# Splits and sums moved from GpSimd to VectorE and ScalarE, g scaled with its clamp, and a new table of places

## The chip, the cores and the metric

The kernel runs on one core of one Trainium2 chip. The metric is the device time of one execution in microseconds. A core has five engines that matter here: TensorE (PE, matrix products; PEld is its loading of weights), VectorE (DVE), ScalarE (ACT), GpSimd (POOL) and SyncE (SP, which issues the transfers). Each takes its instructions in its own program order and waits, where an operand needs it, for another engine's semaphore.

## What is computed

Three blocks in a row: attention in which a query sees only the keys of its own hash bucket (B=2, H=8, S=768, D=64), then a gated block of width 1536, then a block of width 2048 with a piecewise activation. The weights of the last two come as float64.

```python
x = attention(q, k, v, proj)            # 1536 tokens x 512
gate = 1.0 / (1.0 + np.exp(-(x @ w_gate)))
y = gate * (x @ w_val) @ w_out          # d_ff 1536
h = y @ w_in2                           # d_ff 2048
g = np.where(h >= 1, h, np.where(h <= -1, 0.0, (h + 1) ** 2 / 4))
out = g @ w_out2
```

## The kernel before

**Products.** Every product is made of three f16 matmuls: each operand is split into a high half (a cast to f16) and a low half (what the cast left over), and hi·hi, lo·hi and hi·lo are added (lines L420 to L422, for z L1349 to L1351). So each tensor that enters a product costs one cast and one subtraction. The operands are scaled by powers of two first, which are taken from their largest absolute value. For that, a [128,1] maximum goes out to DRAM as a row (`row_out`, L255), comes back as one row, a handful of 1x1 steps make exponents of it (`exponents`, L238 to L248, two on DVE and the rest on POOL), and the result is sent out to all partitions (`row_in`, L260). The float64 weights are loaded raw and converted on chip: absolute value on ACT (L163), then clamp (L166), shift (L169), low word (L172) and sign (L175) on DVE. `w_hl` splits w_out1's and w_out2's chunks (ACT L1114, DVE L1117), `i_hi` and `i_lo` w_in2's (ACT L1152, DVE L1156).

**Stages**, by the span of the profile: attention to about 240 us; the gate and val products as "quads" (seven products for eight, on sums of blocks) to 416; w_out1 of batch 0 to about 470 and of batch 1 to 522, 12 chunks each (`o_mm`); MoE2 of batch 0, 16 chunks (`p_mm`, then `p_act`, then `z_mm`), to 661; MoE2 of batch 1 (called LB) as quads again, eight windows, to 788.

**What touches the change.** `h_hl` splits the gated h: a cast on ACT (L1162) and, on POOL, the subtraction (`xsub`, L130). `y_cp` copies w_out1's output out of PSUM (ACT L1199, DVE L1201; it is called `yf` in batch 0 and `yB` in batch 1), `y_max` takes its maxima (L1208, L1210 writes `v0s`), `y_row` fetches the scale, `y_half` (L1217 to L1221, POOL) makes the factors `usc`, and for batch 1 `y_sc` scales y in place (L1225, POOL, four times 128x768). Then 18 operations on POOL prepare batch 1's right operands: four sums (`y_sum`), seven casts (L152) and seven subtractions (L130), named B11, B21, B22 and T1 to T4. `p_act` makes g of p: relu and square on ACT (L1328, L1330), a clamp on DVE (L1333, `gg`), a scaled cast on ACT (L1338) and a scaled subtraction on DVE (L1341). `Quad2.half` does the same for batch 1 (L1294 to L1305). `g_max` (L208) takes the maxima of w_out1, w_in2 and w_out2 ahead of their use, from raw chunks called `go`, `gi` and `gz`.

**What sets the order.** No scheduler does. Each call is put into a list with a key time by `on(t, fn, ...)`, about one unit to a microsecond of TensorE's work; the list is sorted by the key and run. In the attention, `at` does the same per group of heads. So the tables of key times (AT, AM, QP, WP, YA, ZA, PA, SA, CA and the offsets in the loops) set the order of every engine.

Of the kernel before, what the change touches and what calls it, by code (L numbers as in the profile page):

```python
# [35 lines left out]
def lsh_attention_glu_act(ctx, tc, qt, kt, v, proj, w_gate, w_val, w_out1, w_in2, w_out2, ident_d, code_d, out):  # L36
# [435 lines left out]
    with ExitStack() as actx:  # L472
# [254 lines left out]
        with tc.manual_schedule():  # L727
# [895 lines left out]
```

## Time and profile before

| | us |
|---|---|
| median of 3 runs (lowest, highest) | 793.93 (792.8, 796.42) |
| the profiled execution | 794.84 |
| its span | 793.0 |

Busy time within the span: PE 738.1 us (93%), DVE 666.0 (84%), ACT 527.0 (66%), POOL 303.1 (38%). The mean granted clock of TensorE is 0.988 of full. The profile divides the span by engine, by line and by stretch; a wait of an engine is put down to the instruction of another whose end released it. Since the kernel is a chain of stages with different limits, the views by stretch are read first, then TensorE's waits in a stretch, then the timelines of the engines that it waits for.

### The profile page before, as it was taken

What the parts mean: (1) busy time and instruction counts of PE and PEld (TensorE: products, weight loads), DVE (VectorE), ACT (ScalarE), POOL (GpSimd) and SP (SyncE); (2) the same over time, 40 slices, a digit from 0 to 9 for tenths busy, and PEclk for the clock granted to TensorE, in tenths of its full rate; (3) what the DMA queues carried; (4) which work ended last, traced back from release to release, by engine and by line L of the source; (5) the groups of instructions that cost most, each with busy time, mean ns of one, the idle gap of its engine ahead of it and who ended that gap; (6) DMA issues with size and microseconds to landing.
All of it is one profiled execution on the core that took longest, in us unless ns stands there. A gap on an engine that the chain in (4) does not pass through costs nothing.

```text
span 793.0 us, 13271 instructions
## 1 busy us (share of the span) xinstructions
PE 738.1 (93%) x4883; PEld 460.9 (58%) x4883; DVE 666.0 (84%) x1106; ACT 527.0 (66%) x978; POOL 303.1 (38%) x345
## 2 busy tenths in 40 slices
PE   7899999999989999989898999988689999999997
PEld 4778888888865555555454546644245554455553
DVE  6999998988997798897789989999998895676653
ACT  6889889988866567556373445455357776776764
POOL 6334459754784445355224346306930000000000
PEclk9999999999999999999999999999889999999999
DMA  8656354534112356556568514314123300100002
GB/s 255 178 141 162 91 151 120 140 91 94 53 29 79 97 170 216 162 153 201 169 228 329 189 53 161 103 58 135 51 80 107 107 1 22 58 1 1 1 1 79
DMA packets 53200, 89.59 MB, mean 113 GB/s; under 512 B 9872, under 2 KB 33040, under 8 KB 53136
## 3 DMA queue, kind: packets, MB, share of 16 engines
q1 hardware_dynamic: 52400, 88.07, 36.7%
q8 instruction: 38, 0.62, 0.3%
q10 hardware_dynamic: 736, 0.69, 0.3%
q14 instruction: 26, 0.21, 0.1%
HBM read 68.65 MB, written 3.15 MB: 91 GB/s over the span
## 4 chain that ended last, share of the span: by engine, by line
PE 31%; DVE 23%; ACT 6%; DMA 5%; issue 4%; SPq 1%; POOL 0%; ACTq 0%; DVEq 0%
DMA wr_g<-in_moe_w_gate_dram 2%; DVE wf_o L172 2%; DVE gmx L208 2%; DVE w L172 1%; PE p L422 1%; PE p L420 1%; PE p L421 1%; PE qe L1351 1%; PE qe L1350 1%; PE qa L1350 1%; PE qe L1349 1%; PE qa L1351 1%; PE qa L1349 1%; DVE g L1341 1%; PE o L1350 1%
## 5 line engine op out<-in xcount | busy, mean ns | idle before, releaser
L642 DVE SCALAR_TENSOR_TENSOR PT<-pt,PT 128x512 f16<-128x512 f32 x144 | 95.6, 683 | 9.3 <-ACT PT L639 7.5
L604 DVE TENSOR_REDUCE st<-sc 128x1 f32<-128x768 f32 x96 | 90.9, 949 | 5.7 <-PE sc L596 4.8
L608 ACT ACTIVATE P<-sc,st 128x768 f32<-128x768 f32 x96 | 87.1, 908 | 7.6 <-DVE st L604 6.8
L639 ACT ACTIVATE PT<-pt 128x512 f16<-128x512 f32 x144 | 82.9, 600 | 12.8 <-PE pt L630 11.2
L630 PE MATMUL pt<-ident,P 128*128 128x128 f32 x576 | 80.1, 277 | 0.6 <-DVE PT L642 0.6
L630 PEld LDWEIGHTS pt<-ident,P 128*128 128x128 f32 x576 | 64.4, 140 | 13.6 <-issue 7.8
L130 POOL TENSOR_TENSOR h<-h,h 128x768 f16<-128x768 f32 x24 | 43.5, 1820 | 50.8 <-ACT h L1162 37.8
L708 PE MATMUL O<-PT,vh 128*64 128x256 f16 x576 | 54.3, 277 | 1.7 <-DVE xr L717 1.7
L420 PE MATMUL p<-y,i 128*128 128x384 f16 x128 | 43.3, 338 | 11.9 <-DVE gg L1333 10.0
L422 PE MATMUL p<-y,i 128*128 128x384 f16 x128 | 43.8, 342 | 2.7 <-DVE i L1156 2.6
L421 PE MATMUL p<-y,i 128*128 128x384 f16 x128 | 43.3, 338 | 0.0
L708 PEld LDWEIGHTS <-vh 128*64 128x64 f16 x576 | 31.0, 109 | 14.6 <-issue 13.8
L1338 ACT ACTIVATE g<-gg,usc 128x384 f16<-128x384 f32 x32 | 19.7, 615 | 29.6 <-DVE gg L1333 29.0
L1114 ACT ACTIVATE w<-wf_z,gsc 128x512 f16<-128x512 f32 x16 | 11.6, 724 | 39.7 <-DVE wf_z L175 39.7
L420 PE MATMUL y<-h,w_o 128*128 128x384 f16 x96 | 31.9, 332 | 3.5 <-DVE h L391 3.5
L708 PE MATMUL O<-PT,vl 128*64 128x256 f16 x288 | 33.8, 273 | 0.0
L1351 PEld LDWEIGHTS <-g 128*128 128x128 f16 x192 | 18.8, 98 | 23.8 <-DVE g L1341 1.0
L422 PE MATMUL y<-h,w_o 128*128 128x384 f16 x96 | 32.1, 334 | 0.0
L421 PE MATMUL y<-h,w_o 128*128 128x384 f16 x96 | 31.9, 333 | 0.0
L596 PE MATMUL sc<-N,N 128*128 128x384 f32 x96 | 28.9, 382 | 3.0 <-ACT N L532 1.9
L1114 ACT ACTIVATE w_o<-wf_o,hsc 128x512 f16<-128x512 f32 x12 | 8.7, 724 | 34.6 <-DVE wf_o L175 34.6
L1349 PEld LDWEIGHTS <-g 128*128 128x128 f16 x192 | 19.0, 99 | 21.9 <-ACT g L1338 1.6
(351 smaller groups left out, 2378.3 us busy)
## 6 DMA issues: line engine op xcount, KB each, us to landing
wr_o<-in_moe_w_out_dram SPq DMA_DIRECT2D x28, 512.0 KB, 3.9
gi<-in_moe_w_in_dram SPq DMA_DIRECT2D x21, 384.0 KB, 4.7
gz<-in_moe_w_out_dram SPq DMA_DIRECT2D x21, 384.0 KB, 5.9
go<-in_moe_w_out_dram SPq DMA_DIRECT2D x16, 384.0 KB, 4.7
H<-U SPq DMA_DIRECT2D x28, 192.0 KB, 3.4
wr_i<-in_moe_w_in_dram SPq DMA_DIRECT2D x8, 512.0 KB, 3.9
wr_i<-in_moe_w_in_dram SPq DMA_DIRECT2D x16, 256.0 KB, 3.0
n<-in_qt_dram SPq DMA_DIRECT2D x8, 384.0 KB, 4.3
```

What stands on the lines that cost most here:

```text
L130: eng.tensor_tensor(out=out, in0=a, in1=b, op=ALU.subtract)
L420: nc.tensor.matmul(ps, lhsT=wh, rhs=rh, start=first, stop=False, **kw)
L421: nc.tensor.matmul(ps, lhsT=wh, rhs=rl, start=False, stop=False, **kw)
L422: nc.tensor.matmul(ps, lhsT=wl, rhs=rh, start=False, stop=last, **kw)
L604: nc.vector.tensor_reduce(out=self.st[:, 0, self.c:self.c + 1], in_=self.sc[:, :, 0:HN], op=ALU.max, axis=AX.XY, negate=True)
L608: nc.scalar.activation(out=self.P, in_=self.sc[:, :, 0:HN], func=AF.Exp, bias=self.st[:, 0, self.c:self.c + 1], scale=1.0, accum_out=self. ...
L630: nc.tensor.transpose(self.ps[m][:, j, :], un[2 * self.n + e].P[:, a, c:c + 128], ident)
L639: nc.scalar.activation(out=self.part(0, m), in_=self.ps[m], func=AF.Copy, scale=PSCALE)
L642: nc.vector.scalar_tensor_tensor(out=self.part(1, m), in0=self.ps[m], scalar=PSCALE, in1=self.part(0, m), op0=ALU.mult, op1=ALU.subtract)
L708: nc.tensor.matmul(O_ps[r, 0:GN], lhsT=vv[m][:, e, i * D:(i + 1) * D], rhs=PT[:, l, e * NI + i, :], start=(s == 0), stop=(s == len(steps) ...
L1349: nc.tensor.matmul(OA[b][i], lhsT=gh[:, ts], rhs=wh, start=(fc == ORD2[0]), stop=False)
L1351: nc.tensor.matmul(OA[b][i], lhsT=gl[:, ts], rhs=wh, start=False, stop=(fc == ORD2[-1]))
```

## The change

It does four things.

1. `h_hl` computes the low half on DVE (24 subtractions of 128x768).
2. `y_sum` and the low halves of `y_part` move from POOL to DVE (four and seven of 128x768), the high halves from POOL to ACT (seven casts). `y_sc` stays on POOL.
3. g's scale is put into the relu's and the clamp's factors, so that the cast and the subtraction behind them have no scale operand. The factors are clamped with SMAX, for which `y_half` takes nine small POOL operations, before five.
4. The tables of key times get new numbers nearly everywhere. Beside the tables below, the y operations, which were 4.3 units apart, stand 5.26 apart; the casts and clamps of batch 0's MoE2 are 1.09 units apart, before 0.5.

```diff
@@ h_hl
-            xsub(nc.gpsimd, lo, x, hi)
+            xsub(nc.vector, lo, x, hi)
@@ y_row
-        row_in(("y", b), vmx[b][:, 4:8], 3.0, False, True)
+        row_in(("y", b), vmx[b][:, 4:8], 13.0, False, True)
@@ y_half
-        nc.gpsimd.tensor_scalar(out=usc[:, b, 4:5], in0=usc[:, b, 0:1], scalar1=2.0 ** 20, scalar2=2.0 ** -15, op0=ALU.mult, op1=ALU.max)
-        nc.gpsimd.tensor_scalar(out=usc[:, b, 0:1], in0=usc[:, b, 0:1], scalar1=2.0 ** 15, scalar2=2.0 ** -20, op0=ALU.mult, op1=ALU.min)
...
+        ts(out=u[:, 4:5], in0=u[:, 0:1], scalar1=SMAX, scalar2=1.0, op0=ALU.mult, op1=ALU.min)
+        nc.gpsimd.tensor_tensor(out=x[:, 1:2], in0=x[:, 1:2], in1=u[:, 4:5], op=ALU.mult)
+        ts(out=u[:, 0:1], in0=u[:, 0:1], scalar1=1.0, scalar2=1.0 / SMAX, op0=ALU.mult, op1=ALU.max)
...
@@ y_sum, y_part
-        b_sum(nc.gpsimd, YB, name)
+        b_sum(nc.vector, YB, name)
-            b_hi(nc.gpsimd.tensor_copy, YB, name, q2)
+            b_hi(nc.scalar.copy, YB, name, q2)
-            b_lo(nc.gpsimd, YB, name, q2)
+            b_lo(nc.vector, YB, name, q2)
@@ p_act (and alike in Quad2.half)
-            nc.scalar.activation(out=GG[b, fc][0][:, ns], in_=TT[k], func=AF.Copy, scale=u_sc(b, 0))
+            nc.scalar.copy(out=GG[b, fc][0][:, ns], in_=TT[k])
-            nc.vector.scalar_tensor_tensor(out=gl[:, ns], in0=TT[k], scalar=u_sc(b, 0), in1=gh[:, ns], op0=ALU.mult, op1=ALU.subtract)
+            xsub(nc.vector, gl[:, ns], TT[k], gh[:, ns])
@@ places
-        "v": {"seed": (1.4987, 3.9081, 5.743), "p5": 2.7931, "sum": (4.2578, 6.9331, 7.0596, 8.0394), "act": (4.894, 6.5461, 6.7413, 6.5916)},
+        "v": {"seed": (0.3623, 2.8959, 5.4602), "p5": 2.4313, "sum": (3.0782, 5.7535, 7.5389, 6.9122), "act": (3.7144, 5.3665, 5.5617, 6.5916)},
-        "v": {"load": -13.3839, "abs": (-7.5564, -5.8377), ...
+        "v": {"load": -14.3264, "abs": (-6.6935, -4.8952), ...
-            on(t0 + dt * k + 6.0, g_max, w, k)
+            on(t0 + dt * k + 6.9395, g_max, w, k)
-        for d in (-7.0, -1.8, -1.0, 0.1, 1.2, 2.4):
+        for d in (-7.4031, -2.2031, -0.9659, -0.8198, 0.7594, 1.9072):
-                    on(t0 + YA["max"][i] + (2.3 if b == LB else 0.0), y_max, b, i)
+                    on(t0 + YA["max"][i] + (1.2645 if b == LB else -1.1678), y_max, b, i)
-        on(end + 17.0 + 4.3 * i, y_sum if len(a) == 1 else y_part, *a)
+        on(end + 17.5403 + 5.2568 * i, y_sum if len(a) == 1 else y_part, *a)
```

The order that results is shown at three places. First DVE's own order in w_out1 of batch 0, one step of the loop (`wf_o` is the raw chunk under conversion, `gmx` a maximum of w_out2, `w_o` the split chunk, `h` the low half of h). Before:

```order
L172 SCALAR_TENSOR_TENSOR wf_o_5757<-wr_o_8_5696,wf_o_5757 128x512
L208 TENSOR_REDUCE gmx<-gz_5736 128x1
L175 SCALAR_TENSOR_TENSOR wf_o_5757<-wr_o_8_5696,wf_o_5757 128x512
L166 TENSOR_SCALAR wf_o_5800<-wf_o_5800 128x512
L1117 SCALAR_TENSOR_TENSOR w_o_8_5806<-wf_o_5757,hsc,w_o_8_5806 128x512
L169 TENSOR_SCALAR wf_o_5800<-wf_o_5800 128x512
L208 TENSOR_REDUCE gmx<-gz_5759 128x1
```

After:

```order
L173 SCALAR_TENSOR_TENSOR wf_o_5744<-wr_o_8_5693,wf_o_5744 128x512
L209 TENSOR_REDUCE gmx<-gz_5717 128x1
L131 TENSOR_TENSOR h_8_5783<-h_2_4293,h_8_5783 128x768
L176 SCALAR_TENSOR_TENSOR wf_o_5744<-wr_o_8_5693,wf_o_5744 128x512
L167 TENSOR_SCALAR wf_o_5788<-wf_o_5788 128x512
L209 TENSOR_REDUCE gmx<-gz_5735 128x1
L170 TENSOR_SCALAR wf_o_5788<-wf_o_5788 128x512
L1118 SCALAR_TENSOR_TENSOR w_o_8_5803<-wf_o_5744,hsc,w_o_8_5803 128x512
```

h's low half comes in between L172 and the sign step, and the clamp and shift of the next chunk now stand ahead of the low half of this one. (Lines of the changed kernel are one higher here than those of the kernel before.)

Second, DVE at the start of MoE2 of batch 0, around the last maximum of y (`vmx`, then `v0s`; `gg` is a clamped half of a chunk, `g` its low half). Before:

```order
L1333 SCALAR_TENSOR_TENSOR gg_0_1_6667<-p_0_0_1_6620,usc,t_0_1_6648 128x384
L1208 TENSOR_REDUCE vmx_68<-yB_6576 128x1
L169 TENSOR_SCALAR w_4_6645<-w_4_6645 128x512
L1341 SCALAR_TENSOR_TENSOR g_0_6643<-gg_0_1_6667,usc,g_0_6643 128x384
L1208 TENSOR_REDUCE vmx_68<-yB_6577 128x1
L1210 TENSOR_REDUCE v0s<-vmx_68 128x1
L172 SCALAR_TENSOR_TENSOR w_4_6645<-wr_i_3_6593,w_4_6645 128x512
```

After:

```order
L1209 TENSOR_REDUCE vmx_68<-yB_6580 128x1
L167 TENSOR_SCALAR w_4_6643<-w_4_6643 128x512
L1339 SCALAR_TENSOR_TENSOR gg_0_0_6666<-p_0_0_0_6606,usc,t_0_0_6640 128x384
L170 TENSOR_SCALAR w_4_6643<-w_4_6643 128x512
L1209 TENSOR_REDUCE vmx_68<-yB_6581 128x1
L1211 TENSOR_REDUCE v0s<-vmx_68 128x1
L173 SCALAR_TENSOR_TENSOR w_4_6643<-wr_i_3_6599,w_4_6643 128x512
L1339 SCALAR_TENSOR_TENSOR gg_0_1_6691<-p_0_0_1_6621,usc,t_0_1_6663 128x384
```

The maximum has moved from behind both low halves of chunk 0's g to a place ahead of its second clamp.

Third, the first of y's casts in the same stage. POOL's order before, from the last `y_sc` on (`yB` is y, `pB_y`, `pT_y` and `yT` are its parts and a sum):

```order
L1225 TENSOR_SCALAR yB_6577<-yB_6577,vmx_68 128x768
L152 CAST pB_y<-yB_6571 128x768
L130 TENSOR_TENSOR yT_6846<-yB_6572,yB_6571 128x768
L130 TENSOR_TENSOR pB_y<-yB_6571,pB_y 128x768
L152 CAST pT_y<-yT_6846 128x768
L130 TENSOR_TENSOR pT_y<-yT_6846,pT_y 128x768
```

ACT's order after, around the cast of `pB_y` (`t` is the relu and then the square of one half of a chunk, `g` its high half):

```order
L1334 ACTIVATE t_1_0_6789<-p_0_1_0_6746,usc 128x384
L1153 ACTIVATE i_9_6793<-w_1_6317,gsc 128x512
L1336 ACTIVATE t_1_0_6789<-t_1_0_6789 128x384
L1334 ACTIVATE t_1_1_6805<-p_0_1_1_6773,usc 128x384
L153 CAST pB_y<-yB_6575 128x768
L1336 ACTIVATE t_1_1_6805<-t_1_1_6805 128x384
L1344 CAST g_1_6819<-gg_1_0_6807 128x384
L164 ACTIVATE wf_z_6833<-wr_o_11_6787 128x512
```

The cast has moved from POOL, where only other work on y stood behind it, to ACT, between the relu and the square of chunk 1's second half.

## Rows read from the trace of the kernel before

**Rows 1.** Busy time of each engine by stage (instructions), then PEclk, DMA share, GB/s.

```profile
416.00:470.00 54.00, 47.28 (x271) 26.07 (x269) 48.62 (x75) 19.83 (x29) 20.25 (x14) 0.97 0.54 191
470.00:522.00 52.00, 50.17 (x309) 30.03 (x307) 46.96 (x63) 25.29 (x39) 25.86 (x24) 1.00 0.43 138
522.00:590.00 68.00, 54.37 (x260) 26.38 (x260) 64.65 (x84) 33.41 (x60) 39.19 (x31) 0.92 0.23 73
...
661.00:788.00 127.00, 125.34 (x660) 64.22 (x659) 78.97 (x138) 88.22 (x158) 0.00 (x0) 1.00 0.04 15
```

**Rows 2.** Waits of PE, 521.5 to 604: us in total, times, longest us.

```profile
PE p L420 <- DVE gg L1333: 10.0, 7, 3.6
PE p L422 <- DVE i L1156: 2.6, 5, 1.2
PE p L420 <- ACT yB L1199: 1.9, 1, 1.9
```

**Rows 3.** Waits of PE, 416 to 521.5.

```profile
PE y L420 <- DVE h L391: 3.5, 1, 3.5
PE qa L420 <- ACT w_o L1114: 1.7, 4, 0.5
PE qa L422 <- DVE w_o L1117: 1.4, 5, 0.3
```

**Rows 4.** Waits of PE, 250 to 416.

```profile
PE qb L420 <- ACT qb L385: 7.6, 5, 1.8
PE qa L420 <- DVE h L391: 2.9, 1, 2.9
```

**Rows 5.** Busy time by stretch, 388 to 392 us (columns as in rows 1).

```profile
388.00:392.00 4.00, 4.00 (x16) 2.01 (x15) 3.93 (x9) 1.23 (x3) 0.86 (x2) 0.59 0.33 67
```

**Rows 6.** Timeline of DVE, one w_out1 step: start us, us, engine, line, operation.

```profile
439.71 0.42 DVE L169 TENSOR_SCALAR wf_o<-wf_o 128x512 uint32<-128x512 uint32 x1
440.05 0.55 DVE L208 TENSOR_REDUCE gmx<-gz 128x1 f32<-128x384 f32 x1
440.51 1.67 DVE L172 SCALAR_TENSOR_TENSOR wf_o<-wr_o,wf_o 128x512 uint32<-128x512 uint32 x1
442.10 0.54 DVE L208 TENSOR_REDUCE gmx<-gz 128x1 f32<-128x384 f32 x1
442.57 0.68 DVE L175 SCALAR_TENSOR_TENSOR wf_o<-wr_o,wf_o 128x512 uint32<-128x512 uint32 x1
443.17 0.41 DVE L166 TENSOR_SCALAR wf_o<-wf_o 128x512 f32<-128x512 f32 x1
444.03 0.75 DVE L1117 SCALAR_TENSOR_TENSOR w_o<-wf_o,hsc,w_o 128x512 f16<-128x512 f32 x1 [0.45 <-ACT w_o L1114]
```

**Rows 7.** Timeline of POOL in the same step.

```profile
439.81 1.82 POOL L130 TENSOR_TENSOR h<-h,h 128x768 f16<-128x768 f32 x1 [3.17 <-ACT h L1162]
```

**Rows 8.** Groups of instructions: xcount | busy us, mean ns | idle before us.

```profile
L172 DVE SCALAR_TENSOR_TENSOR wt_g<-wr_g,wt_g 128x512 uint32<-128x512 uint32 x10 | 6.8, 680 | 0.1
L130 DVE TENSOR_TENSOR pB<-xr,pB 128x384 f16<-128x384 f32 x2 | 1.1, 552 | 1.6 <-ACT pB L152 1.6
L1162 ACT CAST h<-h 128x768 f16<-128x768 f32 x21 | 17.2, 817 | 0.0
```

**Rows 9.** Groups of instructions of DVE, 530 to 661 us.

```profile
L172 DVE SCALAR_TENSOR_TENSOR wf_z<-wr_o,wf_z 128x512 uint32<-128x512 uint32 x10 | 8.9, 891 | 0.2
```

**Rows 10.** Timeline of DVE, three reductions for y's maxima in batch 0.

```profile
473.88 2.67 DVE L1208 TENSOR_REDUCE vmx<-yf 128x1 f32<-128x768 f32 x3
```

**Rows 11.** Timeline of ACT ahead of the wait at 522.

```profile
519.78 0.72 ACT L1114 ACTIVATE w<-wf_z,gsc 128x512 f16<-128x512 f32 x1 [4.31 <-DVE wf_z L175]
```

**Rows 12.** Timeline of DVE, the last maximum of y in batch 1.

```profile
535.05 0.16 DVE L1210 TENSOR_REDUCE v0s<-vmx 128x1 f32<-128x4 f32 x1
```

**Rows 13.** Timeline of POOL, first steps of y_half and the four of y_sc.

```profile
544.57 0.19 POOL L1217 TENSOR_SCALAR vmx<-vmx 128x2 f32<-128x2 f32 x1 [2.40 <-DMA vmx<-row]
547.37 4.70 POOL L1225 TENSOR_SCALAR yB<-yB,vmx 128x768 f32<-128x768 f32 x4
```

More of the change, by code (lines that the diff above doesn't have):

```diff
@@ L791, in lsh_attention_glu_act @@
             F0 = {
-                "max": (0.835, 4.6, 5.2, 6.0),
-                "first": (1.1, 1.92, 2.6, 2.62),
-                "split": (2.63, 2.73, 2.83),
+                "max": (0.835, 4.3363, 4.8113, 6.0),
+                "first": (1.1116, 1.92, 2.6321, 2.6521),
+                "split": (2.6621, 2.73, 2.83),
                 "all": (6.1, 6.4068, 6.5068, 7.0145, 8.1, 8.2),
@@ L1021, in lsh_attention_glu_act @@
                 at(11.9 + 0.65 * i, 0, last, a_abs, "v0", i)
-                at(11.7012 + 0.7012 * i, 0, last, a_max, "v0", i)
+                at(10.8628 + 0.7012 * i, 0, last, a_max, "v0", i)
             for i, t in enumerate((13.0012, 13.3012, 13.6012, 13.4, 13.85, 14.0)):
@@ L1301, in half @@
                     GG[LB, fc] = hg(f"g_{LB}_{fc}")
-                nc.scalar.activation(out=GG[LB, fc][0][:, ns], in_=self.T[g], func=AF.Copy, scale=u_sc(LB, 0))
+                nc.scalar.copy(out=GG[LB, fc][0][:, ns], in_=self.T[g])
             else:
                 gh, gl = GG[LB, fc]
-                nc.vector.scalar_tensor_tensor(out=gl[:, ns], in0=self.T[g], scalar=u_sc(LB, 0), in1=gh[:, ns], op0=ALU.mult, op1=ALU.subtract)
+                xsub(nc.vector, gl[:, ns], self.T[g], gh[:, ns])
     MQ = {}
@@ L1417, in lsh_attention_glu_act @@
     }
     WP = {
-        "g1": {"abs": (-1.9247, -3.3264), "conv": (-1.6834, -1.4318, 0.2739, 1.9568, 2.5568, 3.1568), "max": (-4.591, -3.9121), "row": 0.6467, "scale": 9.3724, "sum": (3.7724, 4.5686, 3.894, 5.4372), "hi": (11.5982, 11.5142, 12.813), "lo": (12.1178, 11.9436, 16.9873)},
-        "g": {"load": -12.353, "abs": (-7.6756, -6.6904), "conv": (-6.1199, -4.9135, -4.4544, -4.2764, -3.8844, -0.7025), "max": (-7.453, -7.1422), "row": -4.3568, "scale": 7.9278, "sum": (-0.0892, 0.6448, 0.9769, 2.8813), "hi": (5.6163, 6.2733, 7.84), "lo": (6.301, 10.1819, 8.2001)},
@@ L1421, in lsh_attention_glu_act @@
-        "v": {"load": -13.3839, "abs": (-7.5564, -5.8377), "conv": (-5.2061, -4.9018, -3.2885, -0.7253, -1.0263, 2.9987), "max": (-6.0592, -5.6294), "row": -1.4716, "scale": 9.9234, "sum": (3.1886, 3.5668, 4.6394, 5.0659), "hi": (10.4857, 10.7314, 12.8717), "lo": (11.968, 12.8863, 15.6185)},
+        "g1": {"abs": (-1.9247, -3.3264), "conv": (-1.6834, -1.2227, 2.2696, 1.9568, 2.5568, 2.5305), "max": (-5.2173, -4.5384), "row": 0.0204, "scale": 8.7461, "sum": (3.1461, 4.5686, 3.894, 5.4285), "hi": (11.5982, 11.5142, 12.628), "lo": (12.1178, 11.9436, 16.9718)},
@@ new lines, in lsh_attention_glu_act @@
+        "g": {"load": -12.353, "abs": (-7.6756, -6.6904), "conv": (-6.1199, -4.6189, -4.5466, -4.3686, -4.145, -0.7947), "max": (-7.5452, -5.621), "row": -4.3568, "scale": 7.9278, "sum": (-0.0892, 0.724, 1.0886, 3.3024), "hi": (4.4351, 4.7082, 6.3431), "lo": (4.8041, 8.8601, 7.6451)},
+        "v": {"load": -14.3264, "abs": (-6.6935, -4.8952), "conv": (-4.4301, -3.9593, -2.346, 0.2172, -1.0263, 2.9987), "max": (-6.0592, -5.6294), "row": -1.4716, "scale": 9.9234, "sum": (3.1886, 3.5668, 5.287, 4.3833), "hi": (10.4857, 10.7314, 12.6551), "lo": (11.9836, 12.2806, 15.7582)},
@@ L1452, in lsh_attention_glu_act @@
     end = 14 * NT
-    for w, (t0, dt) in {"o": (30.0, 3.5), "i": (86.0, 3.1383), "z": (154.053, 2.0141)}.items():
+    for w, (t0, dt) in {"o": (29.7834, 3.4864), "i": (86.3431, 3.1293), "z": (154.0638, 2.0141)}.items():
         for k in range(g_num(w)):
             on(t0 + dt * k, g_load, w, k)
-            on(t0 + dt * k + 6.0, g_max, w, k)
-        on(t0 + dt * g_num(w) + 10.0, g_row, w)
-    on(end - 14.0, h_fin)
+            on(t0 + dt * k + 6.9395, g_max, w, k)
+        on(t0 + dt * g_num(w) + 10.3184, g_row, w)
+    on(end - 14.9109, h_fin)
     YA = {
-        "max": (5.0, 6.0, 7.0, 8.0),
-        "row": 14.0,
-        "half": 17.0,
-        "sc": (17.1, 18.1, 19.1, 20.1),
-        "hl": (18.7, 20.3, 22.7, 24.3, 26.7, 28.3, 30.7, 32.3),
+        "max": (5.397, 5.4542, 7.3352, 9.2779),
+        "row": 13.9015,
+        "half": 17.3352,
+        "sc": (17.5648, 18.8514, 22.462, 23.1268),
+        "hl": (21.7268, 22.2728, 22.7, 23.9508, 26.2969, 27.8969, 30.6862, 32.9559),
     }
     def on_conv(fn, m, t0):
-        for d in (-7.0, -1.8, -1.0, 0.1, 1.2, 2.4):
+        for d in (-7.4031, -2.2031, -0.9659, -0.8198, 0.7594, 1.9072):
             on(t0 + d, fn, m, 1)
@@ L1515, in lsh_attention_glu_act @@
     while nconv < 2 * F2:
-        on_conv(w_conv, nconv, end + 0.5 + 5.0 * (nconv - F1 + 1))
+        on_conv(w_conv, nconv, end + 0.5 + 5.3173 * (nconv - F1 + 1))
         nconv += 1
@@ L1546, in lsh_attention_glu_act @@
         zs = ORD2[F2 - 2:] if w == 0 else ORD2[2 * w - 2:2 * w]
-        for i, d in enumerate(ZA[m] if w < F2H else z_at((0.0, 12))):
+        for i, d in enumerate(ZA[m] if w < F2H else z_at((0.9462, 12))):
             on(t0 + d, z_mm, m, zs[i // NI], i % NI)
@@ L1556, in lsh_attention_glu_act @@
         for i, g in ((4, "b"), (5, "c")):
-            on(t0 + PA[m][i] + 1.01, m_op, w, "add", g)
+            on(t0 + PA[m][i] + 1.0537, m_op, w, "add", g)
         for g, ds in CA[m].items():
```

69 lines of the change are left out of this document (37 added, 32 removed), and 12 rows, old and new, of tables (AM, AT).

## The prediction

> **What bounds the kernel now.** I read the busy time by stage first, since the shares over the whole span mix stages with different limits. In the w_out1 stage of the second batch (470 to 522) TensorE has 309 matmuls in 50.17 us of busy time, 0.162 us each, and is idle for only 1.8 us; in the quad windows of the second batch (661 to 788) it is busy for 125.3 of 127 us [rows 1]. There TensorE is the bound, and nothing that VectorE (DVE), ScalarE (ACT) or GpSimd (POOL) does can bring much. The time that can be won lies in three places. In the first batch's w_out1 stage (416 to 470) 271 matmuls at 0.162 us would take 44.0 us, and the stage takes 54: 10 us of loss. From 522 to 590 TensorE is busy for 54.4 of 68 us, at a mean granted clock of 0.92 [rows 1]. Before 416 there are single waits.
>
> The waits of TensorE name the releaser. From 521.5 to 604 they are 10.0 us for DVE's `gg` (the clamp that frees p's bank), 2.6 for DVE's low half of `i`, 1.9 for ACT's copy of `yB` [rows 2]: 14.5 us. From 416 on, 3.5 us stand for the last half of h, and waits for w_out1's split weights come each step [rows 3]. In the gate/val quads 7.6 us wait for ACT's seeds and once 2.9 for DVE's h [rows 4]; after that one the granted clock is 0.59 for 4 us [rows 5].
>
> Why DVE is late is seen in one step of the w_out1 loop. Its seven DVE instructions last 0.42 + 0.55 + 1.67 + 0.54 + 0.68 + 0.41 + 0.75 = 5.02 us [rows 6], and the loop's period is 5.0, where TensorE's 24 matmuls need 3.9. The 1.67 is L172, which takes 0.68 where POOL is still [rows 8]. POOL's subtraction for h runs from 439.81 to 441.63 [rows 7]; L172 starts at 440.51 and ends at 442.18, that is 0.55 after POOL's end. It stood still until POOL was done. The reductions at 440.05 and 442.10 last the same, beside POOL or not [rows 6]. So POOL's long instruction costs DVE's two-input instructions what is left of it. From 547 to 582 POOL works on y without a break, and L172 averages 0.89 over that stage [rows 9]: 10 x 0.21 = 2.1 us too long. Ten groups of DVE instructions stand like this there; with their counts the excess sums to about 20 us.
>
> The Trainium skill ("SBUF — State Buffer", section "SBUF: two separate sides") calls the port pair that DVE and GpSimd share an exclusive lock, held for a whole instruction. The row above agrees: 0.55 us after POOL's end is near the 0.68 of a free one.
>
> **The change part by part.** *h's low part to DVE (24 times 128x768).* The nearest DVE row is the f32-minus-f16 subtraction on 384 columns, 0.552 us [rows 8]; two of these are 1.10, and with part of an instruction's time fixed I take 0.95 (estimate). POOL's 24 x 1.82 vanish. A w_out1 step of the first batch then has on DVE 0.68 + 0.95 + 0.54 + 0.68 + 0.41 + 0.54 + 0.42 + 0.75 = 4.97 us when whole durations are added. But neighbours on DVE overlap: three reductions of 0.95 end within 2.67 us [rows 10], so each starts 0.86 after the last; eight times 0.09 off gives about 4.3. The new order also puts L166, a reduction and L169 between L175 and the weights' low half, so ACT's high half, which DVE waits 0.45 us for now [rows 6], is covered. 0.7 us a step over ten steps would be 7, but of TensorE's loss of 10 us there the 3.5 at 416 and short gaps are not this loop's: some 5 are, of which [rows 3] name 3.1. I take 3.7 us. At 416 the last half of h is held up by POOL in the same way; I take 0.8 of the 3.5. Together **-4.5**, from 0 (if the durations add in full) to -6.
>
> In the second batch's stage the same work lies under TensorE's own. The 1.9 us wait at its end [rows 2] comes from ACT, which stood 4.31 us for a DVE conversion [rows 11] that POOL had delayed: **-2** (0 to -2).
>
> *y's parts.* Of the 18 operations that POOL runs after `y_sc`, four sums and seven low parts go to DVE (11 x 0.95 = 10.4 us), seven casts to ACT (7 x 0.82 by h's cast [rows 8] = 5.7). They are spread one per 5.26 places instead of back to back. Off DVE go the 20 us of stretching. DVE gets lighter by about 10 us in this stage before overlaps, from 64.65 of 68 busy [rows 1].
>
> *g's scale with its clamp.* The cast on ACT and the subtraction on DVE lose their scale operand. Nearest rows: on DVE 0.552 for the plain subtraction [rows 8]; I book 0.07 a time off DVE and 0.1 off ACT, 30 times in the first batch, all hidden. `y_half` grows from five small POOL instructions to nine: from 544.57 to 547.37 the five took 2.80 [rows 13], so four more are 0.8 to 4 us of delay for the first `y_sc`, by which everything of y waits. In the second batch no one is near that.
>
> *MoE2's first batch, summed.* Without the wait at 522, TensorE's loss there is 12.6 of waits [rows 2], the half clock (0.08 below full over 68 us means 10.9 us at the half level, some 5.4 of work lost [rows 1]) and some 3 of short gaps: 21. What stays: about 2 at the first z, which needs DVE's low half of g two us before it can be there; 1 for POOL's four `y_sc`, still 4.70 us long [rows 13]; 1 for DVE, which has little slack per chunk; and a **new wait** of 2.5. In ACT's order the first cast of y stands between the relu and the square of chunk 1's second half. TensorE has p(1,1) ready some 17 us after the stage begins at 522.1. `v0s` comes 13 us after it [rows 12], `y_half` 22.5 and `y_sc` 25.3 [rows 13]; y's last maximum now stands ahead of chunk 0's second clamp instead of behind both its low halves, which I put at 5 us earlier, the four more POOL steps and `y_sc`'s own 1.2 come on top, and I put the first scaled y at 21 to 23. ACT stands 3 to 5 us, behind it are the square that frees p's bank and the next high half of g, and TensorE waits for these. 21 - 6.5 = **-14.5**, between -8 (ACT's stop as long as the whole distance, with the half clock after it) and -18.
>
> *Places in the gate/val quads.* The maxima of w_in2 come 0.94 later after their load, val's weights are loaded 0.94 earlier and val's sums come earlier, so the 2.9 wait and the half clock behind it (0.41 below full over 4 us is 1.6 us of work) should go: **-4** (+2 to -8; the 7.6 us for seeds are the lower end). *Windows and attention:* small shifts, TensorE full: **0** (+1.5 to -1.5).
>
> Sum: -4.5 - 2 - 14.5 - 4 = -25. The profiled execution took 794.84 us (its span 793.0), 0.9 above the median of the runs shown, 793.93; 794.84 - 25 = 769.8, so **770**.
>
> **The rivals.** *(A) No overlap on DVE.* If whole durations add, a w_out1 step is 4.97 against 5.0 now, nothing is won there, and in MoE2 DVE's work per chunk comes to TensorE's own 7.8 us, so that some 5 us more stay: 770 + 4.5 + 5 = 779. For it: dependent neighbours show no overlap, and h's low part sits among such. Against: 2.67 for three [rows 10]. The Trainium skill ("VectorE: DVE Perf Modes", "The DRAIN you can't avoid") says the next instruction does not start until the pipe is empty, which speaks for A; the trace's 0.86 from start to start differs from it, and by the same section one that isn't held starts earlier. Chance 0.17.
>
> *(B) ACT's stop at y is longer.* Every microsecond that the first `y_sc` is later than 23 stops ACT, and through it p's banks. At the low end of the term above, 6 us more: 776. For: in-order ACT, and nine POOL steps ahead. Against: the maxima come earlier. Chance 0.15.
>
> *(C) More goes.* The seeds' 7.6 us and the rest of MoE2's loss vanish too: 770 - 10 = 760. Against: in the quads a DMA brings the weights, and that is as fast as before. Chance 0.12.
>
> *(D) Slower: a new wait in every quad.* The quads' seeds, sums and splits get new places. A seed out of step cost up to 1.8 us by [rows 4] (7.6 in five). In all 23 quads of the new pattern this is 41 us: 770 + 41 = 811. It decides from 25 / 23 = 1.1 us a quad on. Against: order moves there by single places. Chance 0.04.
>
> *(E) The change doesn't do what it says.* If the long DVE instructions come from DMA traffic or their own operands, not from POOL, the stretch stays and 24 x 0.95 + 11 x 0.95 = 33 us come on top, of which 5 fit into DVE's idle time of 470 to 522 and 3 into that of 522 to 590 [rows 1]: 795 + 25 = 820. Against: L172's end follows POOL's to within 0.55 us. Chance 0.02.
>
> **How the numbers follow.** The forecast, 763 to 775, has 0.48, A 0.17, B 0.15, C 0.12, D and E 0.06, and 0.02 are left for no change. The range 757 to 782 holds A, B and most of C, and leaves out D, E, no change, and the far ends of A and C: 0.15 to 0.2. The terms' own ends, all on one side, would reach further, but they need not fall together. Half a per cent (4 us) is about what a measurement of this kernel can tell from no change: faster by more 0.93, within it 0.03, slower 0.04.
>
> **What would show it.** Right: L172 at 0.68 throughout; a w_out1 step near 4.3 us; no ACT wait for `yB` at 522; DVE busy below 62 of 68 us; one ACT wait of 3 to 5 us for POOL's `y_sc`, and waits of TensorE of about 6 us in MoE2's first batch. Wrong: a w_out1 step at 5.0 with every DVE instruction unstretched (A), an ACT stop of over 6 us (B), new waits for seeds in each quad (D), or L172 still at 1.6 with POOL idle (E).

## The result and the profile after

The changed kernel takes 759.81 us (median of four runs, 755.61 to 762.73), the kernel before 793.38 (four runs). The ratio is 0.9565, with a 95% interval of 0.9513 to 0.9618: 33.6 us less. I had forecast 770 within 757 to 782, a gain of 25: sign and range hold, and the gain is 8.6 us larger than forecast. The profiled execution took 759.33 us, with a span of 757.5.

Stage by stage, from the first matmul of each kind on TensorE's timeline to the first of the next:

| stage, us | before | after | difference | forecast |
|---|---|---|---|---|
| start to the first quad matmul | 227.8 | 229.4 | +1.6 | 0 |
| gate/val quads to the first w_out1 matmul | 188.2 | 179.5 | -8.8 | -4 |
| w_out1, both batches, to the first p | 106.1 | 97.4 | -8.7 | -6.5 |
| MoE2 of batch 0, to the first window matmul | 138.8 | 121.2 | -17.6 | -14.5 |
| windows of batch 1 to the span's end | 132.1 | 130.1 | -2.0 | 0 |

The 1.6 us at the start are not the change's: the granted clock of TensorE is at half from 25.2 to 28.6 us of the profile after and nowhere in this stage before, and the run below that leaves every place as it was, and with them the attention, has the same fall and 230.1 us.

Busy time by stretch of the kernel after, columns as in [rows 1]:

```profile
409.00:457.00 48.00, 45.55 (x274) 26.06 (x273) 46.58 (x88) 20.17 (x30) 2.09 (x6) 1.00 0.56 214
457.00:506.00 49.00, 49.00 (x303) 29.50 (x302) 46.58 (x78) 26.31 (x41) 5.70 (x14) 1.00 0.46 151
506.00:574.00 68.00, 65.49 (x351) 34.33 (x349) 63.45 (x114) 45.85 (x84) 8.93 (x17) 0.97 0.31 101
574.00:627.00 53.00, 53.00 (x288) 28.06 (x287) 47.76 (x86) 37.03 (x66) 0.00 (x0) 1.00 0.15 50
```

In the first 68 us of MoE2 TensorE now does 351 matmuls where it did 260 [rows 1], at a clock of 0.97 instead of 0.92. DVE is about as busy as before (63.45 us, before 64.65), but does 114 instructions instead of 84. The waits of TensorE, from the views of 408 to 506 and 506 to 590:

```profile
PE qa L423 <- DVE w_o L1118: 2.1, 6, 0.4
PE y L421 <- DVE h L392: 0.4, 1, 0.4
...
PE qa L1357 <- DVE g L131: 1.8, 1, 1.8
PE qa L1355 <- ACT g L1344: 0.7, 1, 0.7
```

Of the 14.5 us of [rows 2] nothing is left. What stands in MoE2 now is 2.5 us at the first z (the first product with w_out2, which needs chunk 0's g). In the w_out1 stages the 6.6 us of [rows 3] are 2.5. One w_out1 step on DVE's timeline:

```profile
434.02 0.68 DVE L173 SCALAR_TENSOR_TENSOR wf_o<-wr_o,wf_o 128x512 uint32<-128x512 uint32 x1
434.62 0.54 DVE L209 TENSOR_REDUCE gmx<-gz 128x1 f32<-128x384 f32 x1
435.08 0.95 DVE L131 TENSOR_TENSOR h<-h,h 128x768 f16<-128x768 f32 x1
435.95 0.68 DVE L176 SCALAR_TENSOR_TENSOR wf_o<-wr_o,wf_o 128x512 uint32<-128x512 uint32 x1
436.55 0.42 DVE L167 TENSOR_SCALAR wf_o<-wf_o 128x512 f32<-128x512 f32 x1
437.00 0.43 DVE L170 TENSOR_SCALAR wf_o<-wf_o 128x512 uint32<-128x512 uint32 x1
437.34 0.55 DVE L209 TENSOR_REDUCE gmx<-gz 128x1 f32<-128x384 f32 x1
437.81 0.74 DVE L1118 SCALAR_TENSOR_TENSOR w_o<-wf_o,hsc,w_o 128x512 f16<-128x512 f32 x1
438.46 0.68 DVE L173 SCALAR_TENSOR_TENSOR wf_o<-wr_o,wf_o 128x512 uint32<-128x512 uint32 x1
```

The low word's 1.67 us [rows 6] is 0.68, h's low half costs the 0.95 that I took, and the durations sum to 4.99, but the step's period is 438.46 - 434.02 = 4.44: in these rows an instruction starts some 0.08 before the one ahead of it ends. The exception is the one at 437.00, which reads what the one at 436.55 wrote and starts 0.03 after its end.

### The profile page after: what moved, and what is told of

It is laid out like the page before. It is cut to its first block, busy times and chain, and to the rows that moved or that the text cites. A ratio compares the mean times of both kernels' runs of the same rounds, so it can differ in the third digit from the quotient of the medians.

```text
span 757.5 us, 13220 instructions
## 1 busy us (share of the span) xinstructions
PE 728.7 (96%) x4883; PEld 461.5 (61%) x4883; DVE 648.1 (86%) x1141; ACT 521.1 (69%) x985; POOL 227.5 (30%) x311
## 4 chain that ended last, share of the span: by engine, by line
PE 35%; DVE 22%; DMA 4%; ACT 3%; issue 2%; POOL 1%; SPq 1%; ACTq 0%; DVEq 0%; POOLq 0%
DVE h L131 2%; PE p L423 2%; PE p L422 2%; PE p L421 2%; DMA gi<-in_moe_w_in_dram 2%; PE qa L1357 2%; DVE gmx L209 2%; PE qa L1356 2%; PE qa L1355 2%; PE qe L1356 2%; PE qe L1355 2%; PE qe L1357 2%; PE o L1356 2%; PE o L1357 2%; PE o L1355 2%; DVE h L392 2%
## 5 line engine op out<-in xcount | busy, mean ns | idle before, releaser
L421 PE MATMUL p<-y,i 128*128 128x384 f16 x128 | 41.7, 326 | 0.0
L422 PE MATMUL p<-y,i 128*128 128x384 f16 x128 | 41.7, 326 | 0.0
L423 PE MATMUL p<-y,i 128*128 128x384 f16 x128 | 41.7, 326 | 0.0
L1357 PEld LDWEIGHTS <-g 128*128 128x128 f16 x192 | 18.9, 98 | 25.1 <-DVE g L131 2.3
L242 POOL TENSOR_SCALAR row<-row 1x1 uint32<-1x1 uint32 x15 | 5.5, 369 | 91.0 <-DVE row L240 90.9
L1334 ACT ACTIVATE t<-p,usc 128x384 f32<-128x384 f32 x32 | 21.3, 665 | 15.9 <-PE p L423 15.8
L1355 PEld LDWEIGHTS <-g 128*128 128x128 f16 x192 | 18.9, 98 | 21.3 <-ACT g L1344 1.3
L421 PE MATMUL y<-h,w_o 128*128 128x384 f16 x96 | 31.3, 326 | 0.4 <-DVE h L392 0.4
L1356 PEld LDWEIGHTS <-g 128*128 128x128 f16 x192 | 18.9, 98 | 20.5 <-issue 0.8
L423 PE MATMUL y<-h,w_o 128*128 128x384 f16 x96 | 31.3, 326 | 0.0
L422 PE MATMUL y<-h,w_o 128*128 128x384 f16 x96 | 31.3, 326 | 0.0
L597 PE MATMUL sc<-H,H 128*128 128x384 f32 x96 | 28.9, 382 | 2.3 <-ACT P L609 2.2
```

The lines of the kernel that those rows point to most:

```text
L421: nc.tensor.matmul(ps, lhsT=wh, rhs=rh, start=first, stop=False, **kw)
L422: nc.tensor.matmul(ps, lhsT=wh, rhs=rl, start=False, stop=False, **kw)
L423: nc.tensor.matmul(ps, lhsT=wl, rhs=rh, start=False, stop=last, **kw)
L1355: nc.tensor.matmul(OA[b][i], lhsT=gh[:, ts], rhs=wh, start=(fc == ORD2[0]), stop=False)
L1356: nc.tensor.matmul(OA[b][i], lhsT=gh[:, ts], rhs=wl, start=False, stop=False)
L1357: nc.tensor.matmul(OA[b][i], lhsT=gl[:, ts], rhs=wh, start=False, stop=(fc == ORD2[-1]))
```

## The experiments

The theories: **L**, GpSimd's long instructions hold VectorE's two-input instructions, and taking them off brings the time; **P**, the new places bring it. All kernels are put together from the two kernels shown. The stage lengths are from one profile each, the medians from four to six runs. The kernel before was run again with each series (medians of 793.4 to 795.6 us), so totals of different series are best compared by their ratios to it. The stage of the quads, before the first w_out1 matmul, varies between profiles with the same places by up to 7 us; what varies is shown further down.

### The moves and the places apart

h's low part alone:

```diff
-            xsub(nc.gpsimd, lo, x, hi)
+            xsub(nc.vector, lo, x, hi)
```

> The kernel before, with h's low part (24 subtractions of 128x768) on VectorE instead of GpSimd and nothing else. Theory L (GpSimd's long instructions hold VectorE's two-input instructions until they end): L172 falls from 1.67 to 0.68 us in the w_out1 loop, a step has 4.97 us of VectorE work by full durations, about 4.4 with overlap, and the wait for ScalarE's high half (0.45) stays uncovered in the old order, so a step takes about 4.8 instead of 5.0; the stage from the first w_out1 matmul to the first p matmul falls from 106.1 us by 3 to 5 (the 1.9 us wait at its end goes too), MoE2 stays. Total about 790. Rival P (the new places bring the time, the move alone nothing): within 1.5 us of before, the step still 5.0. Rival E (the long VectorE instructions have another cause): L172 stays at 1.6 and 24 x 0.95 us come on top, in the w_out1 loop 10 us: about 803.

789.47 us, ratio 0.9934 (0.9908 to 0.9961). w_out1 goes from 106.1 to 102.1 us, the wait of 1.9 us at its end is gone, MoE2 moves little (138.8 to 136.9). A step on DVE's timeline:

```profile
436.69 0.75 DVE L1117 SCALAR_TENSOR_TENSOR w_o<-wf_o,hsc,w_o 128x512 f16<-128x512 f32 x1 [0.45 <-ACT w_o L1114]
...
438.16 0.68 DVE L172 SCALAR_TENSOR_TENSOR wf_o<-wr_o,wf_o 128x512 uint32<-128x512 uint32 x1
438.76 0.95 DVE L130 TENSOR_TENSOR h<-h,h 128x768 f16<-128x768 f32 x1
...
441.56 0.75 DVE L1117 SCALAR_TENSOR_TENSOR w_o<-wf_o,hsc,w_o 128x512 f16<-128x512 f32 x1 [0.45 <-ACT w_o L1114]
```

L172 is free at 0.68, and the step takes 441.56 - 436.69 = 4.87 us. The 0.45 for ACT is still there. In the changed kernel it is gone, and it is about the way from 4.87 to 4.44: that part belongs to the new order.

All three moves with the old places:

> The kernel before with all three moves (h's low part, y's sums and parts, g's scale) but every place as before. Theory L: the w_out1 stage falls by 3 to 5 us as in the run with h alone, MoE2's first batch (138.8 us from the first p to the first window matmul) falls by 10 to 15, since the 20 us of stretched VectorE instructions go; the quads before (188.2 us) stay. Total 775 to 782. Rival P: under 6 us in all, above 787, since in the old order the y work, one per 4.3 places, meets VectorE's other work and ScalarE stops at casts that wait for y.

781.78 us, 0.9837 (0.9808 to 0.9866), 12.4 less than before in the same series (794.15). w_out1 takes 102.1 and MoE2 129.0 us, just under the gain expected; the quads stay (189.7).

All new places with the old engines:

> The kernel before with every new place, and all work on the engines where it was. Theory L: the gate/val quads win what they win with the whole change (188.2 to about 179.5 us), while the w_out1 stage and MoE2's first batch keep L172 at about 1.6 us wherever GpSimd works: w_out1 106 to 102, MoE2 138.8 to 130 or longer, since GpSimd's y work is now spread over 90 us; total 775 to 785. Rival P: 760 to 766, nearly the whole gain.

782.0 us, 0.9844 (0.9809 to 0.9878), 12.2 less. The quads take 185.5, w_out1 101.0, but MoE2 137.4, hardly less than before. The low word is still held, in w_out1 on average:

```profile
L172 DVE SCALAR_TENSOR_TENSOR wf_o<-wr_o,wf_o 128x512 uint32<-128x512 uint32 x12 | 16.9, 1404 | 0.0
```

So neither L nor P stands alone. Moves and places bring 12.4 and 12.2 us apart, which adds up to 24.6; the change brings 33.6. Some 9 us come only where both are made, and the intervals of the three ratios, taken together, leave about 5 us either way on this figure. 6.4 of it is in MoE2 (9.8 and 1.4 alone, 17.6 together), and that part is firm, since the profiles below that keep MoE2's places and moves have the stage at 120.9 to 121.5 us. The rest is within the scatter of the quads.

The changed kernel with h back on GpSimd:

> The changed kernel with h's low part back on GpSimd. Theory L: L173 1.5 to 1.7 us again where GpSimd's subtraction runs beside it, a w_out1 step of 4.45 us goes to 4.9 or 5.0, the w_out1 stage from 97.4 to 102 to 105 us, the rest as it is: 765 to 768. Rival P: within 2 us of the changed kernel, VectorE's step being shorter by 0.95 us where it doesn't meet GpSimd.

768.36 us, 0.9671 (0.9649 to 0.9694), 8.5 us more than the changed kernel. w_out1 goes back to 102.1, and the low word to 1.6:

```profile
L173 DVE SCALAR_TENSOR_TENSOR wf_o<-wr_o,wf_o 128x512 uint32<-128x512 uint32 x11 | 17.6, 1602 | 0.0
```

MoE2 does not stay as it was, as L had it: it takes 123.8 us. TensorE waits 2.3 and 1.4 us at the first z, where it waited 0.7 and 1.8, and its clock stays at half for longer behind these waits.

The changed kernel with y's work back on GpSimd:

> The changed kernel with y's sums and parts (18 operations) back on GpSimd, at the new places, one per 5.26. Theory L: VectorE's two-input instructions are stretched again where GpSimd works on y, from about 30 us after MoE2's start to its end, some 18 operations of 1.0 to 2.2 us; each costs VectorE up to its rest, about 10 to 15 us in all, against 10.4 us of work taken off VectorE. MoE2's first batch goes from 121.2 to 127 to 132 us, the other stages stay: 766 to 771. Rival P (the spacing was what mattered, back to back before, and not the engine): within 2 us of the changed kernel.

774.7 us, 0.9751 (0.9711 to 0.9791), more than L had put: MoE2 takes 133.8 us. GpSimd's row is 18 operations without a break again (531.5 to 564.8 us, two of the scalings among them), since in its own queue nothing stands between them: places 5.26 apart space nothing on an engine that has no other work. So this run does not test whether spacing alone would help. On DVE's timeline beside it:

```profile
545.32 0.60 DVE L1339 SCALAR_TENSOR_TENSOR gg<-p,usc,t 128x384 f32<-128x384 f32 x1
...
546.41 2.13 DVE L173 SCALAR_TENSOR_TENSOR w<-wr_i,w 128x512 uint32<-128x512 uint32 x1
548.58 1.21 DVE L176 SCALAR_TENSOR_TENSOR w<-wr_i,w 128x512 uint32<-128x512 uint32 x1
549.70 2.17 DVE L131 TENSOR_TENSOR g<-gg,g 128x384 f16<-128x384 f32 x1
551.79 1.86 DVE L167 TENSOR_SCALAR wf_z<-wf_z 128x512 f32<-128x512 f32 x1
```

The plain subtraction of g, 0.555 us when free, takes 2.17. And the hold is not one of two-input instructions alone, as my prediction and L have it: the weights' clamp L167, which has one tensor input, takes 1.86 where it takes 0.42 free. The clamp of p at 545.32, which reads p from PSUM, runs beside GpSimd at its usual 0.6, and the reductions of [rows 6] did too.

### The lock without a reader

```diff
...
             xsub(nc.vector, lo, x, hi)
+            xsub(nc.gpsimd, echo, x, hi)
```

> The changed kernel, and GpSimd does each of h's 24 subtractions once more, into a tile that nobody reads. No engine waits for these results. Theory L: the lock alone brings the loss back, L173 or its neighbours go from 0.68 to 1.3 to 1.7 us, a w_out1 step from 4.45 to over 5.2 us (VectorE keeps its 0.95 too), the w_out1 stage from 97.4 to 105 to 112: 766 to 774. Rival W (what VectorE and TensorE lost was the wait for GpSimd's result): within 2 us of the changed kernel, the step at 4.45.

786.72 us, 0.9899 (0.9865 to 0.9933): 27 us worse than the changed kernel, though nobody reads `echo` (a tile of its own, made ahead of the loop). w_out1 takes 121.2 us, more than expected, since the second batch is hit too. DVE's timeline in the loop, then GpSimd's:

```profile
434.82 1.93 DVE L131 TENSOR_TENSOR h<-h,h 128x768 f16<-128x768 f32 x1
...
439.19 2.13 DVE L173 SCALAR_TENSOR_TENSOR wf_o<-wr_o,wf_o 128x512 uint32<-128x512 uint32 x1
```

```profile
433.66 2.27 POOL L131 TENSOR_TENSOR echo<-h,h 128x768 f16<-128x768 f32 x1 [3.04 <-ACT h L1165]
438.97 1.80 POOL L131 TENSOR_TENSOR echo<-h,h 128x768 f16<-128x768 f32 x1 [3.04 <-ACT h L1165]
```

GpSimd's two end at 435.93 and 440.77; DVE's at 436.75 and 441.32, 0.82 and 0.55 later. It is again the rest of GpSimd's instruction plus most of DVE's own (0.95 and 0.68 when free). In the views of waits from 407 to 529 us no engine waits for any of these copies, so it is not a buffer that the copy holds either. Rival W (the wait for the result) and rival E of the prediction are out: the presence of GpSimd's instruction alone costs it.

### Where the places work

The old places of the quads and of the maxima beside them:

> The changed kernel with the old places of the gate/val quads' seeds, sums, splits and loads and of the maxima that run beside them; all else changed. My prediction put 4 us on these places, the comparison of stages shows 8.7 us less from the first quad to the first w_out1 matmul (188.2 to 179.5). If the places carry it, this stage goes back to 186 to 189 us, with the single waits of 2.9 us for h and 1.8 for seeds, total 766 to 769. If a part of the 8.7 comes from GpSimd's absence at the stage's end (h's first two subtractions) and from how long the transfers happen to take, the stage stays at 181 to 185: 761 to 765.

767.48 us, 0.9662 (0.9633 to 0.969). The quads take 188.2 as before, and the waits are those of [rows 4], in the view of 229 to 420:

```profile
PE qb L421 <- ACT qb L386: 7.0, 4, 3.1
PE qa L421 <- DVE h L392: 2.8, 1, 2.8
```

So the places carry this stage. But its gain is smaller than the profile after makes it look: the four profiles with old places have 186.3 to 189.7 us here (mean 188.1), the ten with new ones 178.5 to 185.5 (mean 182.6). That is 5.5 us, and the profile after was a lucky one. The 2.9 us wait for h is 0.3 in the profile after and at most 1.6 in the other nine.

What varies is for the most part TensorE's clock. The stage in the profile after, then in the run with all new places on the old engines:

```profile
229.40:409.00 179.60, 170.85 (x1066) 101.01 (x1064) 160.24 (x310) 110.33 (x212) 77.63 (x114) 1.00 0.52 166
```

```profile
228.00:413.50 185.50, 175.14 (x1065) 103.87 (x1063) 160.01 (x310) 110.54 (x212) 78.84 (x116) 0.97 0.51 161
```

The clock of 0.97 is some 5 us of work lost in 185.5, and TensorE's waits are only 1.6 us longer (10.1 against 8.5). In the latter the clock fell three times, each time at a single wait of over 2 us, two of them for seeds (a seed is ScalarE's copy of one sum of a quad into the next, on which TensorE goes on adding). The profile after has waits of 2.1 and 2.2 us with no fall behind them, so which wait is followed by one stays open. How long the wait for one seed is hangs on a transfer. ACT's timeline after, and in the run with y four places earlier (its quads took 185.5 too):

```profile
300.51 0.68 ACT L164 ACTIVATE wt_g<-wr_g 128x512 f32<-128x512 f32 x1 [0.36 <-DMA wr_g<-in_moe_w_gate_dram]
301.10 0.47 ACT L386 ACTIVATE qb<-qa 128x384 f32<-128x384 f32 x1
```

```profile
303.55 0.68 ACT L164 ACTIVATE wt_g<-wr_g 128x512 f32<-128x512 f32 x1 [2.42 <-DMA wr_g<-in_moe_w_gate_dram]
304.12 0.49 ACT L386 ACTIVATE qb<-qa 128x384 f32<-128x384 f32 x1
```

The seed stands behind an absolute value that waits for a transfer, 0.36 us in one and 2.42 in the other; TensorE waits 0.58 and 2.20. Behind the 0.58 the granted clock stays at 1.00, behind the 2.20 it is 0.50 from 305.3 to 308.7 us.

The old places of MoE2's five steps on g:

```diff
-                on(ta + 2 * n + 2.8042 + 1.086 * m, p_act, 0, fc, n, m)
+                on(ta + 2 * n + 2.0 + 0.5 * m, p_act, 0, fc, n, m)
```

> The changed kernel with the old places of relu, square, clamp, cast and subtraction in MoE2's first batch (2.0 + 0.5 m instead of 2.80 + 1.09 m). With all moves and old places MoE2's first batch took 129.0 us, with both 121.2, and in the former VectorE waited 7.7 us for ScalarE (for casts, relus and split weights). Theory S (the wider steps bring ScalarE's result before VectorE needs it, and this is what places give in MoE2): 121.2 goes to 125 to 129 us. Rival: the gain is with the other places (weights' conversion at 5.32, y's operations at 5.26), and this one alone is worth under 1.5 us.

769.54 us, 0.9667 (0.9637 to 0.9696). MoE2 takes 128.1 us, 6.8 more than with the change and near the 129.0 of the moves alone. TensorE's waits, 508 to 640, then DVE's, 508 to 600:

```profile
PE p L423 <- DVE i L1157: 4.8, 8, 1.0
PE p L421 <- DVE gg L1339: 3.2, 3, 2.2
...
DVE w L1118 <- ACT w L1115: 3.9, 5, 0.8
DVE gg L1339 <- ACT t L1336: 3.9, 5, 0.8
DVE g L131 <- ACT g L1344: 1.6, 4, 0.6
```

TensorE waits for DVE again, and DVE waits 9.4 us for ACT where it waits 5.3 in an equally long stretch of the changed kernel (506 to 598). These places are the part that needs both: with GpSimd off its back DVE still waits for ACT in the old order. With the new order alone (all new places, old engines) TensorE waits 9.4 us for `gg` in MoE2, with DVE held by GpSimd. These places without the moves were not run apart from the others.

### ScalarE's stop at y

The y operations four places earlier:

```diff
-        on(end + 17.5403 + 5.2568 * i, y_sum if len(a) == 1 else y_part, *a)
+        on(end + 13.5403 + 5.2568 * i, y_sum if len(a) == 1 else y_part, *a)
```

> The changed kernel with the 18 y operations four places earlier. The first cast of y then stands before chunk 1's first relu in ScalarE's order. In the changed kernel ScalarE stood 1.4 us at this cast and TensorE waited for nothing there, where I had put 3 to 5 us and 2.5. Theory B (a stop of ScalarE stops p's banks and TensorE): with some 3 to 5 us of stop, TensorE waits 2 to 6 us for gg or p's relu and MoE2's first batch goes from 121.2 to 124 to 128 us: 762 to 767. Rival: the banks' and g's slack covers it, under 1 us more.

764.14 us, 0.9609 (0.9572 to 0.9647). This missed its aim. At 13.5403 the first cast slipped ahead of the first scaling at 13.5648, so that part of y is cast unscaled and ScalarE waits for nothing. MoE2 takes 121.5 us. It still tells something: without any stop the stage is no shorter than with the changed kernel's stop (121.2). At 14.0403 instead:

> The changed kernel with the 18 y operations 3.5 places earlier, still behind the first scaling of y on GpSimd (in the run with four places the first cast had slipped ahead of that scaling, so it waited for nothing). ScalarE reaches the first cast some 17.5 us after the stage's start, the scaled y is there at 22: a stop of 4 to 5 us, as long as my prediction had it, with chunk 1's relus behind it. Theory B (the stop goes through p's banks to TensorE): waits of TensorE of 2 us or more and the half clock after them, MoE2's first batch from 121.2 to 124 to 128 us. Rival S (the slack of the new places swallows it): under 1 us more.

762.61 us, 0.9597 (0.9569 to 0.9625). The cast in ACT's timeline of the changed kernel, then in this one:

```profile
528.29 0.83 ACT L153 CAST pB_y<-yB 128x768 f16<-128x768 f32 x1 [1.37 <-POOL yB L1231]
```

```profile
532.76 0.83 ACT L153 CAST pB_y<-yB 128x768 f16<-128x768 f32 x1 [3.42 <-POOL yB L1231]
```

With 3.42 us of stop TensorE has one new wait, 1.1 us for `gg`, and MoE2 takes 122.9, 1.7 more, between what theory B and rival S had put. In total time that is not clear of noise. Theory B's mechanism is there at a small price.

### What is left, and g's scale

Two maxima of y later, the third behind g's first low half and the fourth behind its second (the row, the scaling and y's operations move by three places, not shown):

```diff
...
-                    on(t0 + YA["max"][i] + (1.2645 if b == LB else -1.1678), y_max, b, i)
+                    on(t0 + YA["max"][i] + (1.2645 + (0.0, 0.0, 3.0, 2.7)[i] if b == LB else -1.1678), y_max, b, i)
...
```

> The changed kernel with the third and the fourth maximum of y (0.95 us each) behind the first and the second low half of chunk 0's g on VectorE, and y's row, scaling and operations three places later. In the changed kernel TensorE waits 0.7 and 1.8 us at the first z and then runs some 4 us at the half clock; two maxima stand ahead of that low half. Theory Z (these 1.9 us are on the path to the first z): the 1.8 us wait falls under 0.5, no half clock follows, MoE2's first batch 121.2 to 117.5 to 119.5 us, total 756 to 758. Rival: another wait comes last there (ScalarE's cast of g, at 0.7 now), under 1 us less.

760.39 us, 0.9562 (0.9534 to 0.959): no gain. The half clock is gone from the stage's first 68 us (1.00 granted), but TensorE's waits at the first z split instead of falling:

```profile
517.24 0.39 PE L1357 MATMUL qa<-w,g 128*128 128x512 f16 x1 [0.87 <-DVE g L131]
520.36 0.39 PE L1357 MATMUL qe<-w,g 128*128 128x512 f16 x1 [1.00 <-DVE g L131]
```

A maximum now stands between the first low half and the second. Two more waits are new, 0.7 us for `gg` and 0.6 for an absolute value on ACT. MoE2 takes 120.9. No version tried is faster than the changed kernel beyond the noise.

g's scale as it was:

> The changed kernel with g's scale back in the cast and in the low half, and the five small GpSimd operations. I booked this part at nothing, hidden under other work, except for four small GpSimd operations less ahead of the first scaled y. Theory: within 2 us of the changed kernel; VectorE's low half of g 0.62 instead of 0.555 us, ScalarE's cast 0.61 instead of 0.50, the first z some 0.2 us later. Rival: in MoE2's first batch VectorE is the bound, 0.07 a time counts in full and more through ScalarE: 2 to 5 us slower.

760.42 us, 0.9554 (0.9525 to 0.9584): this part of the change is worth nothing, as booked. MoE2 even took 119.2 us in the profile: TensorE waited 1.7 us at the first z, with no wait ahead of it, and the granted clock of the stage's first 68 us is 1.00.

```profile
PE qa L1351 <- DVE g L1341: 1.7, 1, 1.7
PE qe L1351 <- DVE g L1341: 0.2, 1, 0.2
```

```profile
511.00:579.00 68.00, 66.12 (x360) 34.83 (x358) 65.27 (x115) 48.49 (x86) 8.26 (x13) 1.00 0.31 101
```

## Why the prediction was right, and where it was short

**The mechanism** was right: DVE was held by GpSimd and freed, 1.67 to 0.68 us on the low word, and the loop's step came out nearly as I had put it. The new wait of ACT stands where I had put it, but is shorter, and the first z is dearer. The sum of 25 us was made stage by stage; that it is near the 12.4 + 12.2 of moves and places apart is chance. In the profile it lacked 2.2 us in w_out1, 3.1 in MoE2, 2.0 in the windows and 4.8 in the quads, and most of the last is luck of that profile. In the chances there is a slip: D and E are both slower and add up to 0.06, and "slower" was given 0.04.

**w_out1, -4.5 and -2 against -8.7.** The step came out at 4.44 where I had put 4.3 (the dependent pair L167, L170 does not overlap). The mis-sized term is the wait for the last half of h: I took 0.8 of its 3.5 us [rows 3] off, and it fell by 3.1, to 0.4. The move of h alone left it at 2.5, so it was mostly the places. The 1.9 us at the end went as told. Rival A fell with the 4.44: whole durations would have given 4.99 and no gain.

The Trainium skill ("VectorE: DVE Perf Modes", "The DRAIN you can't avoid") would have had A right with its first rule, that the next instruction does not start until the pipe is empty; the trace agrees only for the dependent pair, which starts 0.03 us after the end of the one ahead. The exclusive lock of the Trainium skill ("SBUF — State Buffer", "SBUF: two separate sides") agrees with the rows here, those of the unread copy above all, where VectorE's instructions end 0.82 and 0.55 us after GpSimd's.

**MoE2, -14.5 against -17.6.** I left 6.5 us of loss. ACT's stop was 1.4 us instead of 3 to 5 and cost TensorE nothing instead of 2.5: the scaled y came 22 us after the stage's start, within my 21 to 23, but ACT reached the cast at 20.7 and not at 17 to 18. The relu ahead of it on ACT's timeline shows why:

```profile
526.24 0.67 ACT L1334 ACTIVATE t<-p,usc 128x384 f32<-128x384 f32 x1 [0.26 <-PE p L423]
```

It waited for TensorE, which the first z had held up by about 4 us. I had added the two losses; in part the one hides the other. In the run with g's old scale the first z cost 1.9 us, and ACT reached the cast at 19.3. The nine small steps of `y_half` took 3.35 us, where the five took 2.80 [rows 13]: 0.55 more, under the 0.8 to 4 that I put. Even at 3.42 us of stop the price was 1.7, so rival B's 6 us were far too dear. The 1 us for `y_sc` and the 1 for DVE's small slack show no wait of TensorE either. The first z cost more than my 2: 2.5 of waits, and after them TensorE's clock. Three stretches after those waits:

```profile
517.00:519.00 2.00, 1.74 (x5) 0.64 (x6) 2.00 (x5) 1.83 (x4) 0.00 (x0) 0.50 0.69 216
519.00:521.00 2.00, 2.00 (x8) 0.79 (x7) 1.93 (x6) 0.51 (x1) 0.86 (x4) 0.71 0.13 47
521.00:523.00 2.00, 2.00 (x13) 1.02 (x11) 1.97 (x5) 0.54 (x2) 0.17 (x1) 1.00 0.16 15
```

With 0.50 and 0.71 granted, 1.6 of the first four microseconds' work is lost. I had not counted this. So about 4.1 us of my 6.5 are left, all of it at the first z. And I expected DVE under 62 of 68 us; it is 63.45, for the time saved was filled with more chunks.

**Quads, -4 against -8.8 in the profile** and -5.5 over all profiles: the term was nearly right, the wait for h went as told, and the rest is how transfers and with them TensorE's clock fell. Rival D's waits in each quad did not come. Rival C's 760 is the time that came out, but not for its reason: the seeds' waits (`qb`) are still 3.6 to 6.8 us in the ten profiles with the new places, and only MoE2's loss went.

**Windows, 0 against -2.0.** The new places alone give 1.7 of it (132.1 to 130.4): three short waits of 0.7, 0.7 and 0.2 us in the windows are gone. I had read those and booked them at nothing.

## What to carry to other kernels

Where two engines hold each other off, price an instruction of the one by what it keeps the other from, not by its own length: the subtraction of 1.82 us on GpSimd held a VectorE instruction for some 1 us (1.67 against 0.68), as much as the 0.95 that it takes when VectorE does it. A move to another engine and the order for it are one change: here each alone brought little more than a third of the gain, and the two added up fall short of the whole. Spacing out work in an in-order queue does nothing on an engine that has nothing else to do.

## What the runs showed of the hardware that I had not expected

The granted clock of TensorE fell to 0.50, its lower level, after waits of 0.7 and 1.8 us close together at the first z, and so it did behind nearly the same two waits in the runs with the old quads, with y earlier and with y on GpSimd. In the profile with g's old scale, where the waits there were 1.7 and 0.2 us, it stayed at 1.00, as it did with two maxima later, behind 0.87 and 1.00. So 2.5 us of waits cost about 4.1 and 1.9 cost 1.9. And 24 subtractions on GpSimd that nobody reads cost the w_out1 stage 23.8 us (97.4 to 121.2), some 1 us each. GpSimd's own instruction takes 2.27 us in one case and 1.80 in the next, as if it were held too.
